# The opening of the first attention: the mask pattern made by TensorE instead of through DRAM, and a new order for mask copies, head moves, norms and loads

## The chip, the core and the metric

The kernel runs on one core of a Trainium2 chip. A core has a matrix engine (TensorE, PE in the profile; its weight loads are shown as PEld), three engines for elementwise work (VectorE or DVE, ScalarE or ACT, GpSimd or POOL) and SyncE (SP), which here only issues DMAs. Each engine runs its own queue in order; semaphores order the queues among each other. POOL issues DMAs too, in the same queue as its arithmetic. The metric is the device time of one execution in microseconds; before the change its median is 1165.69 us over three runs.

## The reference, cut to what matters

Two attention layers and two gated layers alternate, all with a residual around a layer norm without parameters. The change touches the first attention only.

```python
B, S, D = 1, 2048, 576;  H = 32;  Dh = 18;  W, dil = 8, 2
def attention(x, wqkv, wo):
    q, k, v = split_heads(layernorm(x) @ wqkv)
    idx  = pos[:, None] - arange(W)[None, :] * dil     # 8 keys per query, every second row back
    mask = idx >= 0
    logits = einsum('bhsd,bhswd->bhsw', q, k[idx]) * Dh**-0.5
    attn = softmax(where(mask, logits, -1e9))
    return (einsum('bhsw,bhswd->bhsd', attn, v[idx])) @ wo
def gated(x, w_in, w_sp, b_sp, w_out):                 # F = 4608
    z = gelu(layernorm(x) @ w_in);  z1, z2 = halves of z
    return (z1 * (w_sp @ layernorm(z2) + b_sp)) @ w_out
x = x + attention(x);  x = x + gated(x);  x = x + attention(x);  x = x + gated(x)
```

## The kernel before, in words

*Rows.* The even rows come first and the odd rows after them (`rows_of`), so a window of eight keys with dilation 2 is eight neighbouring rows. The 2048 rows are 16 row tiles of 128. For the attention they are cut anew into 17 query tiles: one of 128 and sixteen of 120, each with 8 rows of halo before it as keys.

*Projections.* `PG(d, qk, cc, ...)` computes 128 columns of q or k (column block d from 0 to 4; block 4 has q and k together) for 512 rows (row block cc from 0 to 3), five matmuls of 512 columns. The result is evicted into a stage buffer (`stg`, `lent`) that holds q and k of one column block for 1024 rows. When the stage is full, one DMA for each head moves its 18 rows to its place in `QK`, a tile in which four heads lie in the four groups of 32 partitions, eight such groups `g` one after another. These head moves go round the queues of POOL and SP, two to POOL for each on SP in the usual pattern `q2`. `VW(t, hh, ...)` computes half of the values of query tile t, five matmuls of 288 columns.

*Mask.* The 14 spare partitions behind the 18 of each head in `QK` carry a pattern (rows of codes and signs times a large number) for which the product of q and k is very negative outside the window. So one matmul gives masked logits. The pattern has a period of 128 rows, and a different start for the first 8. `build_window_rows` (L115) makes it: POOL fills a scratch tile `R` with constants, DVE computes the bits of the codes and writes them into `R`, three DMAs (`part1`, `part2`) store it to a small DRAM tensor `win_period`, and four DMAs (`load`, L184) read it back transposed into `win_pat`. `fill_window_rows` (L194) copies `win_pat` over one half of the rows of `QK` with four DVE copies of 4096 elements per partition, and two small ones for the start. The copies write all partitions, so a head's move must follow the copy of its place.

*The opening* (L597 to L727, with `li == 0`) is an order written out by hand, engine by engine as the calls stand in the code. `S_` takes the statistics of a row tile on DVE, `R_` the inverse root (an addition on DVE, a power on POOL), `A_` applies the norm on DVE into one of four buffers `ln_xn`. Tiles 0 to 3 are then transposed by TensorE (`T_pe`, L657) with an eviction on ACT, tiles 4 to 15 by a DMA transpose issued on SP (`ln_T`). 46 matmuls of the identity with itself keep TensorE at work until the first tile is there. Projections of row block 0 and of row block 1 follow, with the first values; ACT evicts them.

*The loop.* A step s is a half tile: eight groups of heads, half 0 with heads 0 to 15, half 1 with 16 to 31. `L_mm(s + 1)` computes 16 logits tiles, `EXP` exponentiates them on ACT, `PV(s)` multiplies by the values, and DVE divides by the sums into one of three buffers `o_t`, which a DMA transpose on SP turns (into `oT` or `o_slot`). A table says which projection, value, output product (`WO`), store, statistic and norm stands in which step. Projections of row blocks 2 and 3 that do not stand ahead of the loop (`pre`) are spread over its first steps, one in each; output products begin in step 13. There POOL takes over the norms of the 16 new row tiles (`LN_POW`, `LN_XN`), whose results the gated layer reads. `load_win2a` loads weights of the gated layer into space that was lent to two stages, and so waits for their moves.

## Time and profile before

| | |
|---|---|
| three runs | 1164.6, 1165.69, 1165.92 us; median 1165.69 |
| span of the profiled execution | 1170.2 us, 4.5 us above the median of the runs; its time outside the span is not shown |
| busy | PE 98%, PEld 52%, DVE 47%, ACT 29%, POOL 24% |
| opening | 0 to 44.8 us, when the first logits start |
| loop of the first attention | 50.75 (second half tile) to 126.4 us |
| first gated layer | from 126.4 us |
| DMA share of 16 engines | 0.92 until 12.65, 0.96 from 50.75 to 85.54, 1.07 from 85.54 to 126.4 |

How to read it: in a timeline each row has the start and the length in microseconds, the engine, the line of the kernel, what is written from what, how many instructions were merged, and in brackets the idle time of that engine just before and what ended it. Lines are those of the kernel before. A "q" behind an engine's name is its queue issuing a DMA. The time of a DMA from issue to landing is given for POOL's moves only.

### The profile page before, as it was taken

To read this page: it belongs to the slowest core of one execution; us is meant where nothing else is said; L and a number is where in the kernel's file an instruction comes from. 1 tells how busy PE (TensorE), PEld (TensorE's weight loads), DVE (VectorE), ACT (ScalarE), POOL (GpSimd) and SP (SyncE) were. 2 spreads that over 40 slices of the span, in tenths; PEclk is the share of its full clock that TensorE was granted. 3 is DMA by queue.
4 is the path that set the end of the run, shared out by engine and by line. 5 is a ranking of instruction groups with operands and counts; after the bars stand their busy time and mean duration, and the time that the engine had idled before them with its cause. 6 is when DMAs were issued, how large, how long until landed. Compare 5 with 4: busy or idle time off the path is not lost.

```text
span 1170.2 us, 19968 instructions
## 1 busy us (share of the span) xinstructions
PE 1150.5 (98%) x8163; PEld 612.5 (52%) x8258; DVE 550.0 (47%) x1167; ACT 338.8 (29%) x493; POOL 278.8 (24%) x389
## 2 busy tenths in 40 slices
PE   9999999999999999999999999999999999999998
PEld 5457544444444444457755774444444444444677
DVE  8668598322333332244555886963322223322321
ACT  5589455111100111101247884541011110111000
POOL 4659865000000000001153786640000000000000
PEclk9999999999999999999999999999999999999999
DMA  9599697000000000049646997930000000001332
GB/s 217 119 160 294 193 212 142 23 12 12 12 1 12 12 12 1 6 138 296 169 107 105 204 256 182 242 91 1 12 12 12 12 12 1 12 1 46 111 105 74
DMA packets 183240, 106.45 MB, mean 91 GB/s; under 512 B 135225, under 2 KB 164441, under 8 KB 183149
## 3 DMA queue, kind: packets, MB, share of 16 engines
q1 hardware_dynamic: 170285, 84.85, 31.6%
q0 software_dynamic: 6512, 14.57, 4.8%
q10 hardware_dynamic: 6352, 5.75, 1.6%
q8 instruction: 64, 1.05, 0.4%
q14 instruction: 27, 0.22, 0.1%
HBM read 42.40 MB, written 21.77 MB: 55 GB/s over the span
## 4 chain that ended last, share of the span: by engine, by line
PE 85%; POOL 7%; DMA 3%; DVE 2%; issue 2%; ACT 0%; SPq 0%; POOLq 0%; DVEq 0%; ACTq 0%
PE pg L1055 42%; PE po L1104 12%; PE pz L1031 6%; PE pz1s L1031 6%; PE pzs L907 5%; PE pp L436 4%; PE pz L907 4%; POOL ln_xn L259 4%; PE pv L410 2%; PE O_ps L496 1%; PE pw L557 1%; PE L_ps L473 1%; POOL ln_rstd L582 1%; DMA QK<-stg 1%; DMA o_slot<-o_t 1%
## 5 line engine op out<-in xcount | busy, mean ns | idle before, releaser
L1055 PE MATMUL pg<-Wq,Z 128*128 128x512 bf16 x2260 | 497.9, 379 | 2.5
L1055 PEld LDWEIGHTS <-Z 128*128 128x128 bf16 x2304 | 225.5, 98 | 271.8
L1059 DVE TENSOR_TENSOR g_tmp<-pg,ln_xn 128x512 f32<-128x512 f32 x144 | 99.6, 692 | 421.5 <-PE pg L1055 419.5
L1050 ACT ACTIVATE z1T<-pz 128x1024 bf16<-128x1024 f32 x36 | 34.9, 1021 | 500.8 <-PE pz L1031 500.8
L78 POOL DMA_DIRECT2D wout<-in_B_w_out_dram x4 | 4.3, 1070 | 598.8 <-PE pg L1055 598.8
L1104 PE MATMUL po<-wout,Z 128*128 128x288 bf16 x1152 | 141.4, 286 | 0.0
L482 ACT ACTIVATE P_sb<-L_ps 128x1440 bf16<-128x1440 f32 (+3 forms) x136 | 125.1, 972 | 21.1 <-PE L_ps L473 19.7
L1104 PEld LDWEIGHTS <-Z 128*128 128x128 bf16 x1152 | 112.7, 98 | 28.8
L907 PEld LDWEIGHTS <-xnT 128*128 128x128 bf16 (+1 forms) x800 | 68.7, 98 | 80.0 <-issue 15.5
L1060 DVE TENSOR_TENSOR Z<-g_tmp,z1T 128x512 bf16<-128x512 f32 x144 | 99.7, 692 | 12.2
L956 DVE BATCH_NORM_STATS2 z_st<-zp 128x6 f32<-128x512 bf16 (+1 forms) x160 | 91.0, 617 | 5.1 <-ACT zp L954 4.8
L1031 PEld LDWEIGHTS <-w 128*128 128x128 bf16 (+1 forms) x640 | 53.7, 97 | 74.0 <-issue 13.6
L436 PE MATMUL pp<-xnT,wqk_sb 128*128 128x512 bf16 x341 | 82.2, 382 | 2.5 <-DVE o_t L504 1.3
L259 POOL TENSOR_SCALAR ln_xn<-x_new,ln_mv,ln_rstd 128x576 bf16<-128x576 f32 x32 | 73.3, 2291 | 2.6
L1114 DVE TENSOR_TENSOR x_new<-po,xo 128x288 f32<-128x288 f32 (+1 forms) x64 | 28.8, 455 | 87.4 <-PE po L1104 83.9
L1031 PE MATMUL pz<-xnT,w 128*128 128x512 bf16 (+1 forms) x316 | 66.3, 380 | 0.2
L1031 PE MATMUL pz1s<-xnT,w 128*128 128x512 bf16 (+1 forms) x310 | 64.9, 379 | 0.9 <-issue 0.8
L78 POOL DMA_DIRECT2D QK<-stg x81 | 49.5, 614 | 46.0 <-DVE oT L524 14.8
L907 PE MATMUL pzs<-win2a,xnT 128*128 128x512 bf16 (+1 forms) x235 | 59.9, 364 | 0.4 <-issue 0.3
L907 PE MATMUL pz<-win2a,xnT 128*128 128x512 bf16 (+1 forms) x233 | 58.3, 357 | 0.6 <-issue 0.2
L980 POOL TENSOR_SCALAR Z<-zp,z_mv,z_rstd 128x256 bf16<-128x256 bf16 x32 | 55.7, 1740 | 3.4
L436 PEld LDWEIGHTS <-wqk_sb 128*128 128x128 bf16 x360 | 33.5, 98 | 38.3 <-DVE o_t L504 1.5
(113 smaller groups left out, 936.6 us busy)
## 6 DMA issues: line engine op xcount, KB each, us to landing
xres<-x_new SPq DMA_DIRECT2D x48, 288.0 KB
xo<-xres SPq DMA_DIRECT2D x32, 288.0 KB
wout<-in_B_w_out_dram POOLq DMA_DIRECT2D x4, 1296.0 KB, 8.2
xn_rows<-ln_xn SPq DMA_DIRECT2D x32, 160.0 KB
w<-in_B_w_in_dram SPq DMA_DIRECT2D x16, 256.0 KB
QK<-stg POOLq DMA_DIRECT2D x55, 72.0 KB, 5.2
xo<-xres SPq DMA_DIRECT2D x6, 576.0 KB
QK<-stg SPq DMA_DIRECT2D x39, 72.0 KB
```

What stands on the lines that cost most here:

```text
L78: return eng.dma_start(out=out, in_=in_)
L259: e.tensor_scalar(out=xn[:nrows, 0:D], in0=x_t[:nrows, :], scalar1=mv[:nrows, 0:1], scalar2=rstd[:nrows, 0:1], op0=ALU.subtract, op1=ALU.mult)
L436: nc.tensor.matmul(pp[:, :], lhsT=w, rhs=self.xnT[:, c, cc * 512:(cc + 1) * 512], start=(c == 0), stop=(c == 4))
L482: nc.scalar.activation(out=P_bufs[2 * jp + s % 2][:nk, :, :, 0:nq], in_=Lv[:nk, :, :, 0:nq], func=ACT.Exp, scale=scale)
L907: nc.tensor.matmul(out[:, o0:o0 + n], lhsT=self.xnT[r0:r1, c, r * P:(r + 1) * P], rhs=win2(c)[r0:r1, w0:w0 + n], start=start, stop=stop, t ...
L956: nc.vector.bn_stats(out=st[:, x // 512, :], in_=zp[:, x:x + min(512, w0 + n - x)])
L980: eng.tensor_scalar(out=Z[:, b0:b1, i, :], in0=zv[:, b0:b1, :], scalar1=mv[:, 0:1], scalar2=rstd[:, 0:1], op0=ALU.subtract, op1=ALU.mult)
L1031: nc.tensor.matmul(outs[a_], lhsT=w1[r0:r1, c, sub * P:(sub + 1) * P], rhs=self.xnT[r0:r1, c, q * 512:(q + 1) * 512], start=start, stop=st ...
L1055: nc.tensor.matmul(pg[:, :], lhsT=Z[:, jj, i, sub * P:(sub + 1) * P], rhs=Wq[q][:, i, :], start=(i == 0), stop=(i == NS - 1))
L1059: nc.vector.tensor_tensor(out=tmp[:], in0=pg[:, :], in1=bsp[:, qs], op=ALU.add)
L1060: nc.vector.tensor_tensor(out=uT(jj)[:, sub, qs], in0=tmp[:], in1=z1Ts[jj, sub][:, qs], op=ALU.mult)
L1104: nc.tensor.matmul(acc[hh], lhsT=u_rows(j, i), rhs=wouts[j // NJH][:, j % NJH, hh * 288:(hh + 1) * 288], start=(j == 0), stop=(j == NJ - 1))
```

## The change

What it does, part by part:

- The scratch `R` is laid out with 32 rows per head group, zeros included, and prepared on DVE and POOL (`base`). DVE still computes the bits; the codes are now written by POOL (`codes`, eight short operations), the signs are applied by ACT (`signs`).
- No DRAM tensor any more. `turn` (48 matmuls of up to 16 columns against the identity) transposes `R` into PSUM in the place of the first logits' tile, `turned` copies it out with ACT to 32 partitions (in a buffer that later holds probabilities), `spread_` repeats it over 128 partitions with two matmuls against a replicator matrix, and ACT copies it to `win_pat`. `turn` stands behind the transposes of tile 0, `spread_` behind the second projection group.
- The zeroing of weight rows goes from DVE to POOL. There are 44 warm-up matmuls instead of 46. Tile 1 is normalized by ACT instead of DVE; tile 3's transposes are evicted by DVE.
- The q and k weights and the rows 512 to 1023 are loaded in turn, k's weights first, and the first projections are those of k.
- The six copies of the first half of the mask stand between the norms and statistics of tiles 4 to 11, the four of the second half (which stood in `pre`) behind the statistics of tiles 14 and 15. The power of the root of tiles 10 and 11 now follows, on POOL, the head moves of column block 0, and that of tiles 12 to 15 follows those of block 1.
- The projections of row block 0 are done for k and q in turn as the weights come, those of block 1 after values 2 and 3. The first logits stand behind the values of tile 4 and ahead of those of tiles 5 to 8, which DVE evicts; three projection groups instead of six stand ahead of the loop, so the loop holds 15 instead of 12, two of them in step 0 and the last in step 13 instead of 11.

```diff
 def build_window_rows(self, c, R, rep, pat32):
-        one = self.dram.tile([2, MR, 2 * P + 8], bf16, name="win_period")
...
+        def codes():
+            e = nc.gpsimd
+            e.tensor_tensor(out=uu[:], in0=vf[:, 0:4, 0:2], in1=vf[:, 0:4, 1:3], op=ALU.add)
+            e.tensor_scalar(out=Rf[:, 0, 8:12, :], in0=vf[:, 0:4, 1:2].to_broadcast([P, 4, 16]), scalar1=half, ...)
...
+        def signs():
+            nc.scalar.activation(out=Rf[:, :, 0:8, :], in_=Rf[:, :, 0:8, :], func=ACT.Copy, scale=vf[:, 4, 1:2])
+        def turn(ps):
+            for a in range(2):
+                for b_ in range(2):
+                    for m in range(8):
+                        nc.tensor.matmul(ps[0:32, a, b_ * P + m:(b_ + 1) * P:8], lhsT=R[0:16, a, b_, m, :],
+                                         rhs=self.ident[0:16, 0:16], start=True, stop=True)
+                for m in range(8):
+                    nc.tensor.matmul(ps[0:32, 2, a * 8 + m:a * 8 + m + 1], lhsT=R[32:33, a, 0, m, :],
+                                     rhs=self.ident[32:33, 32:33], start=True, stop=True)
+        def turned(ps):
+            for a in range(2):
+                nc.scalar.copy(out=pat32[:, a, 0:2 * P], in_=ps[0:32, a, 0:2 * P])
+            nc.scalar.copy(out=pat32[:, :, 2 * P:], in_=ps[0:32, 2, 0:16].rearrange("p (a m) -> p a m", a=2))
+        def spread_(ps):
+            for a in range(2):
+                nc.tensor.matmul(ps[:, a, 0:2 * P + 8], lhsT=rep[0:32, :], rhs=pat32[:, a, :], start=True, stop=True)
+                nc.scalar.copy(out=pat[:, a, :], in_=ps[:, a, 0:2 * P + 8])
...
             self.load_wv(nc.sync, 2)
-            x_load(x1[:, 0:4, :], 4, 4, nc.sync)
-            self.load_wqk(nc.sync)
+            self.load_wqk(nc.sync, (0,))
+            x_load(x1[:, 0:2, :], 4, 2, nc.sync)
+            self.load_wqk(nc.sync, (1,))
+            x_load(x1[:, 2:4, :], 6, 2, nc.sync)
+            self.load_wqk(nc.sync, (2,))
             x_load(spare, 8, 4, nc.sync)
...
             S_(0)
             R_(0, 1)
-            S_(1)
-            R_(1, 1)
+            SB(1)
             A_(0)
             T_pe(0)
+            turn(X0)
...
+            PG(0, 1, 0, False)
+            PG(1, 1, 0, False)
+            spread_(X0)
+            F0[0]()
             A_(6, 7)
             T_(6, 7)
-            self.load_pat(nc.sync)
-            S_(9, 10, 11)
-            R_(8, 4)
+            setup_bufs(nc.gpsimd)
+            self.zero_right(nc.gpsimd, ("wo",))
             for f in self.load_win2a(nc.gpsimd)[4:6]:
                 f()
-            S_(12)
-            A_(8, 9, 10, 11)
-            T_(8, 9, 10, 11)
-            self.fill_window_rows(QK, 0)
-            S_(13, 14, 15)
-            order = [(d, 0) for d in range(4)] + [(d, 1) for d in range(4)] + [(4, 0), (4, 1)]
...
+            for d, qk in ((2, 1), (3, 1), (0, 0), (1, 0), (2, 0), (3, 0)):
+                PG(d, qk, 0, False)
+            S_(8, 9)
+            R_(8, 2)
+            F0[1]()
+            A_(8, 9)
+            T_(8, 9)
+            for f in F0[2:]:
+                f()
+            S_(10, 11)
+            RE(10, 2)
+            S_(12, 13)
+            for t in (2, 3):
+                for hh in range(2):
+                    VW(t, hh, False)
+            q2 = (nc.gpsimd, nc.sync, nc.gpsimd)
+            for d in range(4):
+                for qk in (1, 0):
+                    PG(d, qk, 1, False, q2)
+                if d == 0:
+                    RP(10, 2)
+                    A_(10, 11)
+                    S_(14, 15)
+                    RE(12, 4)
+                    for f in F1:
+                        f()
+                if d == 1:
+                    T_(10, 11)
+                    RP(12, 4)
+            PG(4, 0, 0, False, (nc.gpsimd, nc.sync))
+            PG(4, 0, 1, False, (nc.gpsimd, nc.sync))
+            A_(12, 13, 14, 15)
             T_(12, 13, 14, 15)
-            nvw0, nvw = 4, 9
+            VW(4, 0, False)
+            VW(4, 1, False)
+            self.ring = ["PT"]
+            L_mm(0)
+            EXP(0)
+            nvw0, nvw = 5, 9
...
-        pre, pgs = pgs[:6], pgs[6:]
+        npre = 3 if li == 0 else 6
+        pre, pgs = pgs[:npre], pgs[npre:]
         if li == 0:
-            pgs.insert(0, pgs.pop(-2))
+            pgs.insert(3, pgs.pop(-2))
         for k_, (d, qk, cc) in enumerate(pgs):
-            at(k_ if li == 0 else (k_ * PG_END) // len(pgs), PG, d, qk, cc, True, *((q2,) if li == 0 else ()))
+            at(max(0, k_ - 1) if li == 0 else (k_ * PG_END) // len(pgs), PG, d, qk, cc, True, *((q2,) if li == 0 else ()))
```

`RE` is the addition on DVE and `RP` the power on POOL that `R_` did together; `SB` and `SA` are the two parts of `S_`; `F0` and `F1` are lists of the copies that `fill_window_rows` made in one go, for the first and the second half of the rows.

222 lines of the change are left out of this document (113 added, 109 removed).

## The prediction

> **What bounds the kernel now.** I read the page's chain first, then the table of windows over the first attention layer, then the timelines of TensorE, DVE and POOL there.
>
> ```profile
> span 1170.2 us, 19968 instructions
> PE 85%; POOL 7%; DMA 3%; DVE 2%; issue 2%; ACT 0%; SPq 0%; POOLq 0%; DVEq 0%; ACTq 0%
> ```
>
> TensorE bounds the kernel; everything but TensorE on the chain is a place where it had nothing to do. The change touches the opening and the first attention, so I cut those into stages (columns: stretch in us, length, busy time and count of PE, PEld, DVE, ACT, POOL, granted clock, DMA share, GB/s):
>
> ```profile
> 36.50:39.00 2.50, 0.03 (x1) 0.00 (x0) 1.87 (x6) 0.00 (x0) 2.50 (x5) 1.00 0.69 170
> 39.00:44.80 5.80, 5.58 (x28) 2.94 (x32) 1.83 (x4) 0.80 (x2) 5.80 (x11) 0.71 0.74 168
> 50.75:85.54 34.79, 31.76 (x614) 18.84 (x620) 25.14 (x62) 30.11 (x34) 18.40 (x33) 1.00 0.96 137
> 149.00:153.00 4.00, 4.00 (x15) 1.55 (x15) 3.97 (x9) 2.31 (x4) 2.89 (x4) 0.57 0.59 123
> ```
>
> A TensorE that idled 2.5 us gets a granted clock of 0.71 for the next 5.8 us, which costs 0.29 x 5.8 = 1.7 us more; the loop of 34.79 us holds 3.03 us of idle. TensorE's timeline says where (start, length, last bracket the idle before it and what ended it):
>
> ```profile
> 6.43 0.45 PE L661 MATMUL pt<-ident,ln_xn 128*128 128x128 bf16 x5
> 7.70 0.45 PE L661 MATMUL pt<-ident,ln_xn 128*128 128x128 bf16 x5 [0.81 <-DVE ln_xn L654]
> 10.18 0.79 PE L661 MATMUL pt<-ident,ln_xn 128*128 128x128 bf16 x10 [0.19 <-DVE ln_xn L654]
> 12.65 8.80 PE L436 MATMUL pp<-xnT,wqk_sb 128*128 128x512 bf16 x39
> 21.29 1.39 PE L410 MATMUL pv<-wv_sb,xnT 128*128 128x288 bf16 x10
> 22.51 10.96 PE L436 MATMUL pp<-xnT,wqk_sb 128*128 128x512 bf16 x49
> 39.00 2.72 PE L410 MATMUL pv<-wv_sb,xnT 128*128 128x288 bf16 x15 [2.47 <-DVE v_ext L402]
> 51.08 0.56 PE L496 MATMUL O_ps<-v_ext,P_sb 128*128 128x19 bf16 x16
> 56.58 0.39 PE L473 MATMUL L_ps<-QK 32*128 32x120 bf16 x16
> 58.50 0.39 PE L473 MATMUL L_ps<-QK 32*128 32x120 bf16 x16
> 69.69 1.25 PE L436 MATMUL pp<-xnT,wqk_sb 128*128 128x512 bf16 x5 [0.74 <-DVE o_t L504]
> 74.28 1.25 PE L436 MATMUL pp<-xnT,wqk_sb 128*128 128x512 bf16 x5 [0.60 <-DVE o_t L504]
> 84.83 0.55 PE L473 MATMUL L_ps<-QK 32*128 32x120 bf16 x3 [0.43 <-DMA QK<-stg]
> 147.94 1.37 PE L907 MATMUL pzs<-win2b,xnT 64*128 64x512 bf16 x5 [0.97 <-ACT zp L954]
> ```
>
> Three places count: the 2.47 us before 39.00, the logits at 84.83 that wait for head moves of the second half of the rows, and 147.94, where the wait of 0.97 us is followed by the clock of 0.57. Behind the first stand DVE and POOL:
>
> ```profile
> 25.28 4.63 DVE L198 COPY QK<-win_pat 128x4096 bf16<-128x4096 bf16 x4 [2.05 <-DMA win_pat<-win_period]
> 30.04 0.81 DVE L641 BATCH_NORM_STATS2 ln_st<-x_in 128x6 f32<-128x288 bf16 x2
> 31.02 0.77 DVE L641 BATCH_NORM_STATS2 ln_st<-x_in 128x6 f32<-128x288 bf16 x2
> 37.13 1.45 DVE L654 TENSOR_SCALAR ln_xn<-x_in,lnx_mv,lnx_rstd 128x576 bf16<-128x576 bf16 x4 [3.92 <-POOL lnx_rstd L647]
> 15.46 0.72 POOL L647 TENSOR_TENSOR lnx_rstd<-lnx_rstd,neg_half 128x2 f32<-128x2 f32 x1 [0.58 <-DVE lnx_rstd L646]
> 30.85 5.20 POOL L78 DMA_DIRECT2D QK<-stg  x9 [7.84 <-DVE ln_st L641]
> 36.06 1.03 POOL L647 TENSOR_TENSOR lnx_rstd<-lnx_rstd,neg_half 128x4 f32<-128x4 f32 x1
> 37.06 3.60 POOL L78 DMA_DIRECT2D QK<-stg  x6
> ```
>
> The mask pattern reaches DVE at 25.28 after two trips through DRAM; the head moves may only follow the mask copies, so POOL's first starts at 30.85; the root of the last four tiles stands behind nine move issues on POOL, and DVE, which waits 3.92 us for it, evicts TensorE's value tiles late. Behind the other two places stands POOL again:
>
> ```profile
> 82.27 0.51 POOL L78 DMA_DIRECT2D QK<-win2a  x1 [2.63 <-DMA QK<-stg]
> 85.07 0.58 POOL L78 DMA_DIRECT2D win2a<-in_B_w_in_dram  x1 [0.68 <-DMA QK<-stg]
> 85.67 0.60 POOL L582 TENSOR_TENSOR ln_rstd<-ln_rstd,neg_half 128x1 f32<-128x1 f32 x1
> 145.71 1.76 POOL L980 TENSOR_SCALAR Z<-zp,z_mv,z_rstd 128x256 bf16<-128x256 bf16 x1
> ```
>
> From 85.67 to 147.47 POOL normalizes the sixteen tiles nearly without a pause, and its end releases ACT and TensorE at 147.94. POOL could not start earlier: its queue was stuck behind moves that waited for earlier ones to land. So what the change is worth at the layer's end is read from when POOL gets past those moves, not from TensorE's opening alone.
>
> **The change part by part.** Prices: eight projection groups take 21.29 - 12.65 = 8.64, so 1.08 each; two value halves 22.51 - 21.29 = 1.22, so 0.61 each; one tile's statistics 31.02 - 30.04 = 0.98; a norm 1.45 / 4 = 0.36; a POOL issue 5.20 / 9 = 0.58; a mask copy 4.63 / 4 = 1.16; a loop step with one group 58.50 - 56.58 = 1.92. The head moves' landings, first those issued from 30 to 46, then from 70 to 90:
>
> ```profile
> DMA to landing us min/median/max: 3.1/3.7/4.3
> ...
> DMA to landing us min/median/max: 5.4/7.9/8.5
> ```
>
> *Pattern turned.* 48 small matmuls come onto TensorE. The trace has none with 16 rows in and 16 columns out; the nearest row is the one at 51.08 (a weight load and 19 columns each): 0.56 / 16 = 35 ns, so 1.7 us. From above, 48 pairs at the warm-up's pitch would be 5.1 us:
>
> ```profile
> 1.36 4.93 PE L626 MATMUL warm<-ident 128*128 128x128 bf16 x46 [1.36 <-POOL ident L191]
> ```
>
> [...] Not below 48 x 24 ns = 1.2, the logits' 0.39 / 16 at 56.58, which run four abreast. I take 1.7, the row with the likest shape. The two spread matmuls of 264 columns cost half a 512-column matmul each, 0.2; two warm-ups fewer give 0.2 back. *Codes on POOL:* eight short operations now stand before the root of tile 0; at 0.2 us each (estimate: a third of the 0.60 that the root of one column takes at 85.67) they fill 1.6 us from the codes' arrival at about 4.0 and hold that root up by some 0.3, so the first transposes (6.43) slip by 0.3; at 0.6 each it would be 3 us, which I keep for the upper end. The turn lies in the idle of 0.81 before the second transposes, and the 0.19 before the third goes too. Sum of the opening: 1.7 + 0.2 - 0.2 + 0.3 - 1.0 = +1.0 us. ACT takes six small copies, the signs and one norm, some 3 us, beside evictions of 0.59 in each 1.08; the zeroing moves from DVE to POOL, which idled 2.11 before a root: both hide, and what they would cost uncovered is their own 3 and 1 us.
>
> ```profile
> 13.93 0.59 ACT L404 CAST stg<-pp 128x512 bf16<-128x512 f32 x1 [0.68 <-PE pp L436]
> 8.89 0.70 POOL L647 TENSOR_TENSOR lnx_rstd<-lnx_rstd,neg_half 128x2 f32<-128x2 f32 x1 [2.11 <-DVE win_vf L163]
> 13.88 6.71 SPq L266 DMA_TRANSPOSE xnT<-ln_xn  x4
> ```
>
> The loads are cut and reordered on SP with the same bytes; before, nothing waited for them at 12.65, so I cost them at nothing, between -0.2 and +0.5. Four loads and three stores of the pattern vanish from SP and POOL. The transposes of tiles 4 to 7 (6.71 on SP then) go out from about 16, so they are in by 23.
>
> *Mask copies and moves.* Two value halves move behind the first eight groups, so those start at 12.65 + 1.0 - 1.2 = 12.4 and, with the spread and four value halves (2.4), the second column block starts at 23.7. Its first two groups end at 25.9, are evicted by 26.6. DVE has by then, from 12.4, evicted a transposed tile (0.7, as ACT's 0.59 for 512 columns), done six statistics (5.9), six norms (2.2) and the mask copies (4.9): it ends at 26.1, so the copies no longer hold the moves. POOL then issues in order: five moves of block 0 (2.9), the root of tiles 10 and 11 (0.72), five of block 1 (2.9), the root of tiles 12 to 15 (1.03), then block 2. That last root also needs DVE: two norms 0.7, two statistics 1.95 after 30.2, so 33.0 against POOL's own 33.1: a tie. The second move of block 2 (head 15) starts at 26.6 + 2.9 + 0.7 + 2.9 + 1.0 + 0.6 = 34.7 and lands 3.7 later, 38.4.
>
> *New wait.* The first logits now stand ahead of eight value halves and three groups, and need heads 0 to 15 whole. TensorE is there at 25.9 + 8 x 1.08 + 1.22 = 35.8 and waits until 38.4: 2.6 us, in place of 2.47. Everything on TensorE is queued behind it. The same idle should bring the same clock loss, 1.7. DVE's four second-half copies (4.6) and last norms (1.4) end at 39.0, so its value evictions fit behind. The second logits come 0.3 + 8 x 0.61 + 3 x 1.08 + 1.7 = 10.1 later, at 48.5; before, they stood at 50.75 with three groups more done, so at 47.5 like for like: +1.0, the opening's sum; the removed stall is paid back by the new one.
>
> *Loop.* The three groups go into it: 31.76 + 3.24 = 35.0 us to the seventeenth half-tile, 83.5 if nothing waits. The output transposes now stand ahead of the moves on SP, so I let DVE's stalls (0.74, 0.60 and smaller) go. The moves of block 3, which that half-tile needs, follow step 12 instead of 10: 48.5 + 3.0 + 11 x 1.92 + 1.9 + 0.9 = 75.4, against 75.1 before. Their landing is then 7.9 and 8.5 as now, less perhaps 1 us because the output weights load before the queues fill. So the logits clear at about 84.7 (85.54 before), after a wait of 1.2, and POOL starts its sixteen tiles at about 84.9 instead of 85.67. TensorE has 0.97 in hand at the layer's end.
>
> **Sum:** 0.8 us less. On the profiled span 1170.2 that is 1169.4; the span lies 4.5 above the median of the runs, 1165.69, so 1164.9.
>
> **The rivals.** *Faster:* the first logits wait under a microsecond (moves landing at 3.1, POOL's chain 1 us shorter), and the clock stays. Then the loop starts at 48.5 - 1.6 - 1.7 = 45.2, block 3's moves 3.3 earlier, and POOL with them, of which I leave 0.6 to the full DMA queues: 0.8 + 3.3 - 0.6 = 3.5 less, 1162.2. For it: the loop's waits of 0.74 and 0.60 left its clock at 1.00. Against it: POOL's twelve issues in series. [...]
>
> *Slower, POOL shut out by the copies.* Four second-half copies of 1.16 now run on DVE exactly while POOL does the last root and block 2's issues. In the trace before POOL idles in both sets of copies, so no row shows them side by side; POOL's six issues beside DVE's norms took 3.60, 0.60 each, against 0.58. If POOL stood still in three of the four, head 15 would land 3.5 later, the second logits stand at 52.0, block 3's moves start at 78.9, and the end is 3.5 - 0.8 = 2.7 above before: 1168.4. It decides from 3.1 us of delay, where the end is 2.3 above. [...]
>
> *Slower, the turn is dear:* 48 at 107 ns are 3.4 more, so the end is 3.4 - 0.8 = 2.6 above before, 1168.3; if the narrow matmuls also let the clock fall, 1.7 more, 1170.0.
>
> *No effect:* the DMA queues (share 0.96 over the loop) hold 85.5 whatever precedes: 1165.7, inside my forecast.
>
> **Chances.** Forecast 0.40 (its own range 1163.4 to 1168.0), faster 0.30, shut out 0.18, dear turn 0.10, others 0.02. About 0.2% (2.3 us) is what a measurement of this kernel can tell from no change: faster by more 0.33, within 0.37, slower by more 0.30. The range reaches to both sides' cases: 1161.2 to 1169.5.
>
> **What will show it.** The turn's busy time on TensorE (1.7); the idle before the first logits and what ended it (2.6, a head move); clock below 1 in the 5 us behind; POOL's issues beside the second-half copies (0.58, or over 1 us if shut out); the wait of the seventeenth half-tile (1.2); POOL's first root of the loop (84.9); the wait at the layer's end. Wrong: if head 15 lands before TensorE gets there, or if POOL's loop start differs by over 2 us.

## The result, and the profile after

The changed kernel takes 1180.26 us (median of four runs, 1178.99 to 1182.6) against 1165.81 us for the kernel before beside it: a ratio of 1.0112, with a 95% interval from 1.0092 to 1.0132. That is 13.1 us (0.0112 x 1165.81) slower, where I had forecast 1164.9 and a range that ended at 1169.5.

The profiled execution of the changed kernel took 1178.99 us, its span 1177.2. The first lines of the page and the shares of the chain:

```profile
span 1177.2 us, 20161 instructions
PE 1160.6 (99%) x8306; PEld 614.8 (52%) x8306; DVE 555.4 (47%) x1174; ACT 338.9 (29%) x493; POOL 285.7 (24%) x390
...
PE 89%; POOL 6%; DVE 2%; DMA 1%; issue 1%; ACT 0%; SPq 0%; POOLq 0%; DVEq 0%; ACTq 0%
```

TensorE has more of the chain (89% against 85%), POOL a little less: the new time is spent where TensorE sets the pace, or where it works at a lower clock. The table over the stretches with a low clock, the first logits and the loop (columns as in the prediction):

```profile
9.80:13.20 3.40, 3.40 (x27) 2.49 (x22) 2.73 (x7) 2.07 (x4) 2.52 (x4) 0.50 1.12 306
40.58:45.54 4.96, 1.29 (x17) 0.55 (x17) 3.69 (x7) 1.52 (x2) 4.96 (x8) 0.84 0.77 137
43.94:50.76 6.82, 5.72 (x24) 3.50 (x25) 1.91 (x5) 1.94 (x2) 6.59 (x12) 0.50 0.85 159
56.66:91.13 34.47, 34.08 (x624) 19.58 (x617) 26.42 (x64) 29.71 (x33) 18.44 (x34) 1.00 0.76 123
730.00:733.40 3.40, 3.40 (x10) 1.28 (x9) 3.37 (x8) 1.78 (x3) 2.22 (x4) 0.50 0.69 158
```

There are three places at a granted clock of 0.50: one window of 3.4 us behind the opening's idle, two (6.82 us) at the first logits, and one at 730, in the layer behind the second attention, which the change doesn't touch. The loop is nearly free of idle (34.47 - 34.08 = 0.39 us). TensorE's timeline at the places of the prediction:

```profile
8.45 0.45 PE L704 MATMUL pt<-ident,ln_xn 128*128 128x128 bf16 x5 [2.02 <-DVE ln_xn L697]
8.83 0.48 PE L185 MATMUL L_ps<-ident,oT 16*32 16x16 bf16 x13
9.87 1.38 PE L426 MATMUL pv<-wv_sb,xnT 128*128 128x288 bf16 x5
15.01 2.32 PE L452 MATMUL pp<-xnT,wqk_sb 128*128 128x512 bf16 x10
18.28 0.27 PE L198 MATMUL L_ps<-P_sb,oT 32*128 32x264 bf16 x1 [0.74 <-ACT win_pat L199]
28.47 10.95 PE L452 MATMUL pp<-xnT,wqk_sb 128*128 128x512 bf16 x50 [0.89 <-DMA xnT<-ln_xn]
40.58 0.35 PE L489 MATMUL L_ps<-QK 32*128 32x128 bf16 x12
41.87 0.50 PE L489 MATMUL L_ps<-QK 32*128 32x128 bf16 x2 [0.94 <-DMA QK<-stg]
44.02 0.28 PE L489 MATMUL L_ps<-QK 32*128 32x128 bf16 x1 [1.65 <-DMA QK<-stg]
45.32 0.28 PE L489 MATMUL L_ps<-QK 32*128 32x128 bf16 x1 [1.02 <-DMA QK<-stg]
56.32 0.40 PE L489 MATMUL L_ps<-QK 32*128 32x128 bf16 x16
```

And DVE's and POOL's, first in the opening, then around the head moves:

```profile
7.96 0.43 DVE L697 TENSOR_SCALAR ln_xn<-x_in,lnx_mv,lnx_rstd 128x576 bf16<-128x576 bf16 x1 [1.47 <-POOL lnx_rstd L680]
5.09 0.63 POOL L162 TENSOR_SCALAR oT<-win_vf 128x64 bf16<-128x64 f32 x1
5.80 0.61 POOL L164 TENSOR_SCALAR oT<-win_uu 128x64 bf16<-128x64 f32 x1
7.35 0.58 POOL L680 TENSOR_TENSOR lnx_rstd<-lnx_rstd,neg_half 128x1 f32<-128x1 f32 x1
38.29 4.63 DVE L207 COPY QK<-win_pat 128x4096 bf16<-128x4096 bf16 x4
31.70 3.03 POOL L78 DMA_DIRECT2D QK<-stg  x5 [5.03 <-DVE ln_st L665]
38.49 2.20 POOL L680 TENSOR_TENSOR lnx_rstd<-lnx_rstd,neg_half 128x4 f32<-128x4 f32 x1
40.37 5.15 POOL L78 DMA_DIRECT2D QK<-stg  x6
45.52 5.01 POOL L78 DMA_DIRECT2D QK<-win2a  x9
91.13 0.60 POOL L598 TENSOR_TENSOR ln_rstd<-ln_rstd,neg_half 128x1 f32<-128x1 f32 x1
```

The codes hold the root of tile 0 until 7.35, DVE and TensorE wait for it, and the clock falls behind that wait. The moves start at 31.70, not at 26.6. Beside DVE's second-half copies (38.29 to 42.9) the root of four columns takes 2.20 us instead of 1.03 and a move's issue 5.15 / 6 = 0.86 instead of 0.58. POOL's moves end at 50.5 (45.52 + 5.01), and its first root of the loop is at 91.13, 5.5 us behind the 85.67 of before.

The spans of the two profiled executions differ by only 7.0 us, the runs by 13.1. So one question of the experiments was where the first layer's loss comes from, and another where the rest is.

### The profile page after: what moved, and what is told of

Same layout as the page of the kernel before. It is cut to its first block, busy times and chain, and to the rows that moved or that the text cites. A ratio compares the mean times of both kernels' runs of the same rounds, so it can differ in the third digit from the quotient of the medians.

```text
span 1177.2 us, 20161 instructions
## 1 busy us (share of the span) xinstructions
PE 1160.6 (99%) x8306; PEld 614.8 (52%) x8306; DVE 555.4 (47%) x1174; ACT 338.9 (29%) x493; POOL 285.7 (24%) x390
## 3 DMA queue, kind: packets, MB, share of 16 engines
q8 instruction: 65, 1.06, 0.4%
## 4 chain that ended last, share of the span: by engine, by line
PE 89%; POOL 6%; DVE 2%; DMA 1%; issue 1%; ACT 0%; SPq 0%; POOLq 0%; DVEq 0%; ACTq 0%
PE pg L1122 42%; PE po L1171 12%; PE pz L1098 6%; PE pz1s L1098 6%; PE pp L452 5%; PE pzs L974 5%; PE pz L974 4%; POOL ln_xn L275 3%; PE pv L426 3%; PE O_ps L512 2%; PE pw L573 2%; PE L_ps L489 1%; DMA QK<-stg 1%; POOL ln_rstd L598 1%; POOL QK L78 1%
## 5 line engine op out<-in xcount | busy, mean ns | idle before, releaser
L426 PE MATMUL pv<-wv_sb,xnT 128*128 128x288 bf16 x340 | 53.4, 300 | 0.0
```

What stands on the lines that cost most here:

```text
L426: nc.tensor.matmul(pv[:nk, 0:288], lhsT=self.xnT[:, c, k0_(t):k0_(t) + nk], rhs=wv_sb[:, c, hh * 288:(hh + 1) * 288], start=(c == 0), stop ...
```

## The experiments

Ratios are to runs of the kernel before on the same chip, with their 95% interval. "First root" is the start of POOL's first root in the first attention's loop, the number of the prediction that stands for the first layer.

**Three suspects in the changed kernel, one at a time.** My first theories were the codes on POOL (A), the second-half copies beside POOL (B) and the lack of cover behind the first logits (C).

```diff
         def codes():
-            e = nc.gpsimd
+            e = nc.vector
...
-            codes()
             signs()
...
             A_(0)
+            codes()
             T_pe(0)
             turn(X0)
```

> The eight code operations go from POOL, ahead of tile 0's root, to DVE, behind tile 0's norm. Theory A (these operations, 0.2 to 0.6 us each on POOL, hold the root of tile 0 up and so cause the idle of 2.02 us and the half clock behind it): the root starts near 5.0 instead of 7.35, the first transposes at 6.4 to 6.7 instead of 8.45, no granted clock of one half near 9.8, the first projection at 11.5 to 12.6 instead of 15.01, and the run is 2 to 4 us shorter than the changed kernel. Rival (DVE is the late one there: eight operations more on it hold the statistics up, and the turn waits for them): first transposes at 6.5, but idle of 1 us or more before the turn and behind it, first projection not before 13.5, end 0 to 1.5 us shorter.

Measured: ratio 1.0071 [1.0047, 1.0095]; first transposes at 6.95, but first projection only at 14.51, and first root at 90.14. TensorE's timeline in this kernel: the idle before the transposes fell from 2.02 to 0.53 us.

```profile
6.95 0.45 PE L703 MATMUL pt<-ident,ln_xn 128*128 128x128 bf16 x5 [0.53 <-DVE ln_xn L696]
...
10.23 0.71 PE L703 MATMUL pt<-ident,ln_xn 128*128 128x128 bf16 x5 [0.82 <-ACT ln_xn L693]
```

And yet the clock behind it, in the table over 9.70 to 13.00:

```profile
9.70:13.00 3.30, 2.77 (x18) 2.15 (x19) 2.40 (x6) 2.14 (x5) 2.50 (x5) 0.50 1.12 300
```

It was halved all the same. A holds for the root and misses the projection, which the rival has. At the first logits TensorE, 0.6 us earlier, waits 4.0 us instead of 3.6, and the second logits stand at 56.11 instead of 56.32: what the opening gave was lost there. The runs are 4.1 us shorter by their medians (1176.2 against 1180.26) and the first root only 1.0; the two intervals overlap, and where the rest would come from is not shown.

```diff
                     RE(12, 4)
-                    for f in F1:
-                        f()
...
             A_(12, 13, 14, 15)
             T_(12, 13, 14, 15)
+            for f in F1:
+                f()
```

> The four mask copies of the second half go on DVE from ahead of the last four norms to behind them. Theory B (a copy on DVE shuts POOL out): the root of tiles 12 to 15 takes 1.0 to 1.1 us instead of 2.20, the first issues of block 2 take 0.58 each instead of 1.1 to 1.5, head 15's move starts near 40.3 and lands near 43.4 instead of 45.3; first logits whole 1.8 to 2.2 us earlier; the end 1.8 to 4 us shorter (the larger value if one window of half clock goes with it). Rival (the landing is set by the DMA queues, which are fed from two issuers): issues shorten, but head 15 lands at 45 all the same, end within 0.7 us of the changed kernel.

Measured: ratio 1.0088 [1.0043, 1.0133], first root 90.75. POOL's timeline:

```profile
39.40 1.03 POOL L680 TENSOR_TENSOR lnx_rstd<-lnx_rstd,neg_half 128x4 f32<-128x4 f32 x1
40.40 3.52 POOL L78 DMA_DIRECT2D QK<-stg  x6
43.91 7.63 POOL L78 DMA_DIRECT2D QK<-win2a  x9
```

The root is back at 1.03 and the six issues at 0.59 each; the nine behind them, which now run beside the copies, take 0.85 each instead of 0.56. So B's effect is shown, but it only moved along the queue. In this execution the opening was 1.1 us later (clock low from 8.32 to 15.15), and the last of the first logits, at 46.32 instead of 45.32, gained nothing. The same root took 2.20 us beside the copies and 1.03 away from them, longer by about one copy (4.63 / 4 = 1.16).

```diff
-            self.ring = ["PT"]
-            L_mm(0)
-            EXP(0)
             nvw0, nvw = 5, 9
...
-                VW(t, hh, li == 0)
+                VW(t, hh, False)
...
-            if k_ == 0 and li > 0:
+            if k_ == 0:
```

> The first logits go back behind the eight value halves of tiles 5 to 8 (which ACT evicts now, since DVE is still busy with copies). Theory C (the wait for head 15 is a matter of cover: 4.9 us of value work lie right behind it): no wait of over 0.5 us at the first logits, no half clock from 44 to 51, second logits at 49 to 50 instead of 56.32, POOL's first root of the loop 5 to 7 us before 91.13, end 5 to 7.5 us shorter than the changed kernel. Rival (POOL's sixteen normalizations are held by the DMA queues in the loop, not by TensorE's progress): second logits early, but waits for moves appear in the loop, and POOL's first root comes no more than 2 us earlier.

Measured: ratio 1.0108 [1.0077, 1.0139], first root 89.42. The first logits ran without a wait, at 45.27, and the second ones took their place. Two of their five waits on TensorE's timeline:

```profile
52.43 0.31 PE L489 MATMUL L_ps<-QK 32*128 32x128 bf16 x2 [0.76 <-DMA QK<-win2a]
53.41 0.42 PE L489 MATMUL L_ps<-QK 32*128 32x128 bf16 x2 [0.68 <-DMA QK<-win2a]
```

And the table over the stretch behind them:

```profile
54.56:57.97 3.41, 3.41 (x9) 1.06 (x7) 1.21 (x3) 1.05 (x2) 0.00 (x0) 0.50 0.37 125
```

With a granted clock of 0.50 there, C is right for the one place, and worth 1.7 us at the first root, not 5 to 7 (the runs show no gain clear of their intervals): the whole stream of moves is late, and here the next logits waited for it.

The three edits together, that is the three diffs above:

> The three edits together (codes on DVE behind tile 0's norm, second-half mask copies behind the last norms, first logits behind the value halves). If A, B and C hold and add up to where other work binds: first projection near 12, second logits at 45 to 46.5, POOL's first root of the loop at 80 to 83, end 9 to 12 us below the changed kernel, that is 3 us above to 3 us below the kernel before, since before it stood like for like at 47.5. Rival (the loop's DMA queues bind): second logits at 45 to 47, but POOL's first root at 85 to 86, as in the kernel before, end within 1 us of before.

Measured: ratio 1.0086 [1.0066, 1.0107], first root 89.01 instead of 80 to 83. All three theories together explain 2.1 of the 5.5 us. They had to be replaced.

**The narrow turn and the clock.** In the kernel with the codes on DVE, the body of the turn:

```diff
-                        nc.tensor.matmul(ps[0:32, a, b_ * P + m:(b_ + 1) * P:8], lhsT=R[0:16, a, b_, m, :],
-                                         rhs=self.ident[0:16, 0:16], start=True, stop=True)
...
+            for k_ in range(12):
+                nc.tensor.matmul(ps[:, a, j * P:(j + 1) * P], lhsT=self.ident[:], rhs=self.ident[:], start=True, stop=True)
```

> The kernel with the codes on DVE, in which twelve matmuls of 128x128 stand in the place of the turn's 48 narrow ones; the mask pattern isn't computed, so the mask rows are wrong. With the codes on DVE the idle before the first projection had shrunk to 0.53 and 0.82 us, and the half clock from 9.68 to 13.09 stayed. Theory A2 (the narrow matmuls of the turn, 16 rows by 16 columns, count as idle for the clock): no granted clock of one half before 15 us, first projection at 12.6 to 13.3 instead of 14.51. Rival (the idle of 0.5 and 0.8 us does it): half clock at the same place, first projection at 14 or later. For the end both theories say little, since the moves behind it are late for another reason: 0 to 2 us below the kernel with the codes on DVE.

Measured: ratio 1.0064 [1.0048, 1.0080], first projection 13.77, first root 90.09. No half clock in the opening, although TensorE idled longer than with the narrow turn. Its timeline:

```profile
6.95 0.45 PE L698 MATMUL pt<-ident,ln_xn 128*128 128x128 bf16 x5 [0.81 <-DVE ln_xn L691]
7.24 0.83 PE L184 MATMUL L_ps<-ident 128*128 128x128 bf16 x12
...
10.21 0.45 PE L698 MATMUL pt<-ident,ln_xn 128*128 128x128 bf16 x5 [1.24 <-ACT ln_xn L688]
```

And the same stretch of the table, with the clock at 1.00:

```profile
9.70:13.00 3.30, 2.38 (x26) 1.81 (x27) 2.38 (x6) 3.04 (x8) 2.50 (x5) 1.00 1.12 309
```

All four runs have a mean clock of 0.997, against 0.994 to 0.996 with the narrow turn. With the narrow turn, TensorE was busy for 2.60 of the 3.41 us ahead of the half clock:

```profile
6.26:9.67 3.41, 2.60 (x60) 1.84 (x58) 3.23 (x17) 1.15 (x3) 1.13 (x4) 1.00 1.01 300
```

That is more than the 2.38 of 3.30 us at which the wide turn kept its clock. So in this pair the half clock goes with the turn's narrow matmuls, on top of short waits, and not with TensorE's busy time. The projection was 0.5 us later than expected, for the longer waits. Again the opening's gain doesn't reach the loop.

**The order and the turn, each alone.** Theory D: the order cuts the stream of head moves. First the changed opening with the order of before from tile 8 on (the loop's own lines are those of before too):

```diff
             T_(6, 7)
+            spread_(X0)
+            S_(9, 10, 11)
+            R_(8, 4)
...
+            A_(8, 9, 10, 11)
+            T_(8, 9, 10, 11)
+            for f in F0:
+                f()
+            S_(13, 14, 15)
+            order = [(d, 0) for d in range(4)] + [(d, 1) for d in range(4)] + [(4, 0), (4, 1)]
```

> The changed kernel's opening with the turned pattern, but from tile 8's statistics on the order of the kernel before (norms of tiles 8 to 11 ahead of the first mask copies, second-half copies and the last value halves behind the fourth group of block 2, six groups ahead of the loop). Theory D (the late end comes from the order: roots on POOL, transposes on SP and the second-half copies cut the stream of head moves, which runs from 31.4 to 50.5 instead of from 30.2 to 45.7): the moves issue without a pause but for one root, from 30 to 46; POOL's first root of the loop at 86 to 87.5 instead of 91.13; end 3 to 5 us below the changed kernel. Rival (the loss is made in the opening, where TensorE's second column block starts at 28.5 instead of 22.5, and stays): POOL's first root at 90 or later, end within 1.5 us of the changed kernel.

Measured: ratio 1.0078 [1.0060, 1.0097]; the first root at 86.53, as D has it; POOL's moves start at 32.96, later than expected, with one root between them, and end at 49.96, hardly before the 50.53 of the changed kernel. The first logits ran at 45.26 without a wait, the second ones waited 0.97 us. The runs gained 4.0 us on the changed kernel (0.0034 x 1166), within D's 3 to 5, but are still 9.1 us (0.0078 x 1166.6) slower than the kernel before.

Then the opening of before with the changed order:

```diff
+            for d, qk in ((0, 1), (1, 1), (2, 1), (3, 1), (0, 0), (1, 0), (2, 0), (3, 0)):
+                PG(d, qk, 0, False)
+            S_(9)
+            R_(8, 2)
+            A_(8, 9)
+            T_(8, 9)
+            for f in F0:
+                f()
+            S_(10, 11)
...
```

From there to the end of the loop it is as the changed kernel.

> The opening of the kernel before (pattern through DRAM, its loads), with the changed kernel's order from tile 8's norms on: copies and moves ahead of the norms of tiles 10 to 15, second-half copies beside the moves, first logits ahead of the value halves, three groups ahead of the loop. Theory D: the stream of moves starts near 30.5 and ends near 49.5, and POOL's first root of the loop comes at 89 to 91 instead of 85.67, the end 3 to 5 us above the kernel before. Rival (the opening is the cause): POOL's first root at 87 or earlier, end at most 1.5 us above the kernel before.

Measured: ratio 1.0063 [1.0046, 1.0080], 7.3 us slower than the kernel before; first root 92.18, later than in the changed kernel. Its TensorE is at the first logits 3.5 us earlier than in the changed kernel and is through with them 1.3 us later. From its timeline:

```profile
37.10 0.63 PE L481 MATMUL L_ps<-QK 32*128 32x128 bf16 x7
39.23 0.46 PE L481 MATMUL L_ps<-QK 32*128 32x128 bf16 x3 [1.50 <-DMA QK<-stg]
...
46.59 0.28 PE L481 MATMUL L_ps<-QK 32*128 32x128 bf16 x1 [2.32 <-DMA QK<-stg]
```

The table over 40.41 to 50.65:

```profile
40.41:50.65 10.24, 5.19 (x23) 2.92 (x24) 4.67 (x10) 2.05 (x2) 9.98 (x16) 0.50 0.78 143
```

And POOL's timeline:

```profile
38.36 2.18 POOL L657 TENSOR_TENSOR lnx_rstd<-lnx_rstd,neg_half 128x4 f32<-128x4 f32 x1
40.23 5.15 POOL L78 DMA_DIRECT2D QK<-stg  x6
```

POOL has the same root at 38.4 and the same issues as in the changed kernel, whose TensorE came from a quite different opening: the stream of moves sets the end of these logits, and TensorE only waits more or less for it. The clock is at one half for 10.24 us, but TensorE was busy for only 5.19 of them, so that costs 2.6 at most; the rest is waiting. D stands as far as the whole order goes: alone it makes a first-layer loss as large as the changed kernel's. Which part of the order costs how much, these runs don't separate.

Then the turn with the order of before throughout, placed where it was meant to hide (the codes are on DVE; against the kernel before, cut):

```diff
             S_(3)
             R_(2, 2)
+            codes()
+            signs()
             A_(2, 3)
             T_pe(2)
             T_pe(3)
             VW(1, 1, False)
+            turn(X0)
+            turned(X0)
...
                 PG(d, 1, 0, False)
+                if d in (1, 2):
+                    spread_(X0, (d - 1,))
                 PG(d, 0, 0, False)
```

> Order of the kernel before throughout, with the pattern turned by TensorE: codes on DVE where they stood before, the turn behind tile 1's last value half, the two spread matmuls a group apart so that no copy of ACT is waited for. Theory D with A2: TensorE's second column block starts at 24 to 25 (22.5 before plus the turn's 1.0 and the spread's 0.5; 1.7 more if the turn costs the clock), the mask copies start at 23.5 instead of 25.3 and the moves at 28.5 to 29, the wait of 2.47 us before the values is under 0.7, the clock stays; the first step of the loop at 48.5 to 50 instead of 51.08; end 0 to 2.5 us below the kernel before. Rival (the head moves of block 3 and the full DMA queues hold the loop's middle whatever precedes): loop starts as early, but POOL's first root at 85 to 86 as before, end within 0.5 us of before; or, if the narrow turn halves the clock and the wait stays, 1 to 3 us above before.

Measured: ratio 1.0053 [1.0034, 1.0072], 6.2 us slower, although its first layer was better than that of the kernel before: no wait before the values, first root at 83.71. In its trace it is 3.6 us ahead of the profile before at 600, and level with it at 760. What it had won was lost from 690 on: 1.9 us by the last roots of the second attention, and 1.7 in a window of half clock from 722.84. In the opening the clock was at one half from 9.45 to 12.87, ahead of the turn, which starts at 13.94. The 3.41 us ahead of that window:

```profile
6.04:9.45 3.41, 1.58 (x19) 1.14 (x18) 3.27 (x12) 1.06 (x2) 1.06 (x2) 1.00 0.97 295
```

There is no narrow matmul in them, only waits of 1.01 and 0.82 us; so here the half clock came without narrow matmuls. The variant with less work ahead of tile 0 lost as much:

```diff
-            bits_()
...
             S_(0)
...
             A_(1)
+            bits_()
             T_pe(1)
...
+            for _ in range(12):
+                nc.tensor.matmul(warm[:, 0:P], lhsT=self.ident[:], rhs=self.ident[:], start=True, stop=True)
```

> The kernel with the turn hidden, with DVE's bit operations moved from ahead of tile 0's statistics to behind tile 1's norm, and twelve idle matmuls where TensorE waits for tiles 2 and 3. In the kernel with the turn hidden the first transposes stood at 7.32 behind idle of 1.01, the clock was half from 9.45 to 12.87 and the projections began at 16.22. Theory: first transposes at 6.3 to 6.6, no half clock before 20, projections from 14.0 to 14.8, POOL's first root of the loop at 82 to 83.3 instead of 83.71 (85.67 before), end 1.5 to 3.5 us below the kernel with the turn hidden, that is within 1.5 us of the kernel before or below it. Rival (DVE's chain of statistics and norms sets the mask copies and with them the moves, whatever TensorE does): projections earlier, but copies at 24.5 and moves at 29.5 as now, POOL's first root at 83.5 or later, end within 1 us of the kernel with the turn hidden.

Measured: ratio 1.0053 [1.0035, 1.0071], first root 83.37. No half clock in the opening, the first transposes at 6.43, but tiles 2 and 3 later, projections at 15.70: the rival has the copies and the end.

**The same two kernels again.** Both unchanged, for a second profile:

> The kernel before, unchanged, for a second profile. Its first profile has a span of 1170.2, while most of its runs take 1164.4 to 1167.2 at a mean clock of 1.0. Theory E (whether a wait of 0.8 to 2.5 us halves the clock for 3.4 us is chance, and so is the wait at the end of the second attention): this profile has no half clock at 40 or at 149, the second logits come 1.7 us earlier, the span is 1163 to 1167. Rival (the wait of 2.47 us always halves the clock): half clock from 40 on again, second logits at 50.7 again, and the difference of the runs lies elsewhere.

> The changed kernel, unchanged, for a second profile. Theory E for it: the idle of 2.02 us before the narrow turn and the 3.6 us at the first logits are long enough to halve the clock every time: half clock again near 9.8 and for two windows near 44, POOL's first root of the loop within 0.5 us of 91.13; only the third place, 730, may be gone. Rival (all is chance): one or more of the first two places without half clock, POOL's first root 1.5 us or more earlier.

Measured: the kernel before took 1169.27 us, with the half clock from 40.46 to 43.87 again behind a wait of 2.56 us, none at 149, and its first root at 84.65. The changed kernel took 1179.47, with two windows of half clock at the first logits again and its first root at 91.92. In the opening its transposes ran at half pace again, but this time from the first ones on (0.71 us for five at 8.45, where the first profile has 0.45), so ahead of the turn; the granted clock of this profile reads 1.00 from 8 to 15 all the same. Both places of the changed kernel come back in TensorE's pace, and in the kernel before the clock at 40 came back too; 149 and 730 did not. For 40 to 44 Theory E stays open: both profiles have the window, but of 29 runs of the kernel before beside the last kernels 15 have a mean clock of 1.0, which leaves none that the clock's record shows. The padded kernel below, nearly the same code, waited only 1.06 us there, kept its clock, and had its first root at 80.26.

The second profiles also divide the loss. Their spans differ by 10.2 us: 7.3 stand at the first root, 8.1 at the first root of the second attention's loop, 10.0 at its last.

**Where the other half is.** At the end of the second attention POOL waits for the last rows, whose stores go through DRAM. All profiles up to here with the turn in them, but that with the late copies, waited longer there. One thing of the change does reach so far: the turn adds 48 pairs of matmul and weight load to TensorE's code, with the spread and two warm-ups fewer some 100 instructions. The page counts a queue of kind "instruction" with 64 packets of 16 KB in the kernel before (1.05 MB) and 65 in the changed one; over the 8163 + 8258 matmuls and weight loads that the profile before counts that is one for 257 of them. Theory F: this queue brings TensorE's code, and 100 instructions more move every later fetch, and one of them into that wait. The test adds such instructions to the kernel before and does nothing else:

```diff
-            for _ in range(46):
+            for _ in range(61):
+                nc.tensor.matmul(warm[0:16, 0:16], lhsT=self.ident[0:16, 0:16], rhs=self.ident[0:16, 0:16], start=True, stop=True)
+            for _ in range(35):
                 nc.tensor.matmul(warm[:, 0:P], lhsT=self.ident[:], rhs=self.ident[:], start=True, stop=True)
```

> The kernel before with 100 TensorE instructions more and no other change: of its 46 warm-ups 35 stay, and 61 narrow ones of 16 rows and 16 columns, of about the same length together, stand ahead of them. Theory F (TensorE's code comes in 16 KB fetches, one for some 250 instructions of matmul and weight load; the turn's 100 instructions shift all later fetches, and at the end of the second attention one lands where stores of the last rows have to get through): the first layer as in the kernel before, but the code fetch at the end of the second attention moves into the wait behind the last rows (51 to 53 us after the first root of that loop instead of 47.7 and 60.7), the last two pairs of roots come 1 to 2 us later (57.3 to 58.5 instead of 56.5), the runs 2 to 5 us above the kernel before. Rival (chance): roots at 56.5, runs within 1 us of the kernel before.

Measured: ratio 1.0035 [1.0016, 1.0053]: 4.1 us slower (1.9 to 6.2), with the same work. The edit is not quite code alone: behind the narrow warm-ups the first five transposes took 0.74 us instead of 0.45. The profiled execution is one of the fastest of its twelve (1167.76 of 1167.49 to 1176.89), with its first root 4.4 us ahead of the second profile of the kernel before and its end only 1.5 us ahead. POOL's timeline at the last roots of that loop, with the wait before them:

```profile
703.48 1.08 POOL L582 TENSOR_TENSOR ln_rstd<-ln_rstd,neg_half 128x1 f32<-128x1 f32 x2 [7.38 <-DVE ln_rstd L581]
```

The queues that were busy in that wait (packets, MB, share of 16 engines):

```profile
q1 hardware_dynamic: 2532, 1.31, 65.4%
q8 instruction: 1, 0.02, 0.8%
```

The same two views of the kernel before, where no fetch falls into the wait:

```profile
707.77 1.08 POOL L582 TENSOR_TENSOR ln_rstd<-ln_rstd,neg_half 128x1 f32<-128x1 f32 x2 [5.04 <-DVE ln_rstd L581]
```

```profile
q1 hardware_dynamic: 1976, 0.87, 64.7%
```

And of the changed kernel, with a fetch in it:

```profile
712.84 1.08 POOL L598 TENSOR_TENSOR ln_rstd<-ln_rstd,neg_half 128x1 f32<-128x1 f32 x2 [6.77 <-DVE ln_rstd L597]
```

```profile
q1 hardware_dynamic: 1975, 1.34, 76.5%
q8 instruction: 1, 0.02, 1.6%
```

The counter-test takes 66 instructions out of the changed kernel, with the same warm-up work:

```diff
-            for _ in range(44):
-                nc.tensor.matmul(warm[:, 0:P], lhsT=self.ident[:], rhs=self.ident[:], start=True, stop=True)
+            for _ in range(11):
+                nc.tensor.matmul(warm[:].rearrange("p (r x) -> p r x", x=P), lhsT=self.ident[:],
+                                 rhs=self.ident[:, None, :].to_broadcast([P, 4, P]), start=True, stop=True)
```

> The changed kernel with 11 warm-ups of 512 columns in place of 44 of 128, the same work in 66 TensorE instructions less. Theory F: the first layer as in the changed kernel (POOL's first root of the loop at 91 to 92), but code fetches at the second attention's end back near 47 and 58 to 60, the roots there at 56 to 56.6 instead of 57.7 and 58.5, the runs 2 to 4 us below the changed kernel's 1179 to 1182. Rival (chance): the runs as the changed kernel's.

Measured: ratio 1.0075 [1.0056, 1.0093] instead of 1.0112: 4.3 us of the loss are gone, with the first layer no better (first root 92.95). The wait before the last roots, and the queues in it:

```profile
712.12 1.07 POOL L598 TENSOR_TENSOR ln_rstd<-ln_rstd,neg_half 128x1 f32<-128x1 f32 x2 [4.29 <-DVE ln_rstd L597]
```

```profile
q1 hardware_dynamic: 1534, 0.71, 59.5%
```

Over the 17 profiles of this study, that wait was 4.29 to 5.07 us in the seven without a fetch of this queue in it, and 6.41 to 7.77 us in nine of the ten with one (4.50 in the tenth, the kernel with the copies late). And a second loss follows: in six of the nine profiles with the longer wait a window of half clock begins between 706 and 731, worth 1.7 us (half of its 3.4), and in none of the eight others. F holds, as far as the shift of the code goes: three kernels moved by 4.1, 4.3 and 5.8 us (the third below) the way that it says, each with an uncertainty of 2 to 3 us. The padded kernel's trace itself shows 2.3 of its 4.1 us, in the wait; it has no such window. How the fetch lengthens the wait is not shown; what the profiles show is that the wait of another engine, with such a fetch in it, was 1.3 to 3.5 us longer in nine of ten.

The same trim, by the same lines, in the kernel with the turn hidden, and then with POOL's two selects on the pattern cut out of `base()` as a function of their own:

```diff
             R_(1, 1)
+            self.win_select()
             A_(0)
```

> The kernel with the turn hidden, its warm-ups trimmed in the same way. Theory F with D: first layer as that kernel's (POOL's first root of the loop near 83.7, 1 to 2 us ahead of the kernel before), no loss at the second attention's end, so the runs 0 to 3 us below the kernel before, where they were 6 above. Rival (chance there, or the profile of the first layer isn't typical): runs 3 us or more above the kernel before.

> The kernel with the turn hidden and the warm-ups trimmed, in which POOL's two selects on the pattern go behind the root of tile 1, so that DVE's bit operations aren't slowed beside them (one took 1.06 us instead of 0.28). Theory: tile 0's statistics start at 3.6 instead of 4.53, the first transposes at 6.4 instead of 7.32, no half clock before 15, projections from 14.0 to 14.6 instead of 16.22; POOL's first root of the loop at 82 to 83.3; runs 1 to 4 us below the kernel before. Rival (the mask copies and moves don't follow, as when the bit operations alone were moved): first root at 83.4 or later, runs within 1 us of the trimmed kernel.

Measured: ratios 1.0003 [0.9991, 1.0014] and 1.0001 [0.9989, 1.0014]; first roots at 85.12 and 81.94. The trim took away 5.8 us (1.0053 to 1.0003), and with it all that was left of the loss. But neither is faster than the kernel before. The first of them missed its first root of 83.7; its first transposes ran at half pace (0.71 us). The second has its first transposes at 6.68 and its projections only at 15.37. Its first root is 2.7 us ahead of the nearer profile of the kernel before, but both of those executions were slower than that kernel's median, so this is no gain in the runs. DVE's chain of statistics and norms has its mask copies start at 24.9 in the last of them, hardly before the 25.28 at which they could start with the pattern through DRAM, so there was little for the turn to win, and what I expected of the earlier selects (1 to 4 us below) did not come.

## Why the prediction was wrong

By its own sign the prediction failed in the first layer: POOL's first root of the loop stood at 91.13 instead of 84.9, 6.2 us off where it allowed 2. Most of the rest of the loss lies at the end of the second attention and just behind it, where it had no term at all.

The sum of the loss: the order alone is 7.3 us (5.4 to 9.3), the code shift alone 4.1 (1.9 to 6.2), and of the 13.1 measured (10.7 to 15.4) 1.7 would remain for the turn's opening. That is less than these intervals, and the parts don't simply add: the turn with the order of before is 9.1 us slower, 5.0 more than the code shift. The wait for the moves hides much of the opening's delay: with the order alone TensorE came to the first logits 3.5 us earlier and left them 1.3 us later.

*Pattern turned, as a price:* too dear in time, too cheap in effect. 48 matmuls took 9.87 - 8.83 = 1.04 us instead of 1.7, but the clock fell behind them. With the codes on DVE it fell behind the narrow matmuls (0.50) and not behind twelve wide ones in their place (1.00); in the changed kernel a wait of 2.02 us stands in front of them too, and the share of each is not shown. The rival of the dear turn (107 ns each, the warm-ups' 4.93 / 46, during which the granted clock reads 1.00) named that and gave it 1.7 us, which is what a window of 3.4 us at one half costs; I gave it one chance in ten.

*Codes on POOL:* 0.61 and 0.63 us for the two wide ones instead of 0.2, so the root came 2.4 us later, not 0.3. My upper end (0.6 each) held it. Eight operations of one engine don't have one price; I took that of a single column for 64. The first projection stood at 15.01 instead of 12.4.

*The second column block at 23.7:* it started at 28.47. The 2.6 us of the opening, 0.74 for ACT's copy between the two spread matmuls, which work on one PSUM tile, and 0.89 for the last transposes of these rows (SP issues them until 24.7) are 4.2 of these 4.8. I had costed the spread as matmuls only, and the transposes as in by 23.

*Copies no longer hold the moves, POOL in series:* this is the step that failed most. The rival "shut out" was right in its effect (a root of 2.20 us beside the copies instead of 1.03, the first three issues 1.1 to 1.5), and it came out on top of a stream that began 5 us later than I had it. What I had not seen is that the last move that the next logits need decides, not the first. The first logits need heads 0 to 15, whose moves come out of `stg`. In the kernel before, POOL had issued these by 40.66, with one root among them; in the changed kernel by 45.52, with two roots and the copies among them, while SP did the transposes of tiles 10 and 11 between its own. And the values and groups that covered this wait before now stand behind it: with the turn and the order of before the whole stream ended as late (49.96), but the first root came 4.6 us earlier. Later copies only slowed POOL's later moves (0.85 us an issue instead of 0.56), and the logits behind the values left the wait to the next logits.

*New wait of 2.6 us with the same clock loss of 1.7:* it was 0.94 + 1.65 + 1.02 = 3.6 us, and two windows with 5.72 us of work in them, so up to 2.9. "The removed stall is paid back by the new one" was the wrong sentence: the old one stands in front of work that the moves don't need and costs one window; the new one grows when TensorE gets there earlier (7.3 us of waiting with the order alone).

*Loop of 35.0 us without stalls:* nearly right. From the second logits at 56.32 to the seventeenth half-tile at 90.16 it is 33.8, and POOL's start follows that half-tile as I had it (after a wait of 0.73 instead of 1.2). But it began 7.8 us later than 48.5.

*The sum against the profiled execution:* I carried its 4.5 us over the median along as if it were in both. Part of it is clock: of 29 runs of the kernel before beside the last kernels, 15 have a mean clock of 1.0, which leaves no recorded window of 3.4 us at one half, while the four runs of the changed kernel show 0.994 to 0.996 (a window of 3.4 us at one half takes 1.7 / 1167 = 0.0015 off the mean). What I booked as the same 1.7 in both is there in every run of the changed kernel, and in the kernel before in some.

*What was not in it at all:* the code. I costed the turn's instructions on TensorE at their own time, beside what they delay there, and not as 100 instructions that stand in front of 16,000 others. The runs give it 4.1 us. No rival held that, and the range couldn't.

## What to carry to other kernels

A transfer stream that feeds the next stage is costed by the last transfer that this stage needs: list every instruction that its issuing queues do before that one, ask what waits for it rather than for the first, and which work stands ahead of that wait to cover it. The kernel before with 100 TensorE instructions more was 0.35% slower (4.1 us, 1.9 to 6.2) for the same work, and what its trace shows of it is a wait behind stores through DRAM, 7.38 us with a fetch of the "instruction" queue in it instead of 5.04 without one in the kernel before; so for a small loss far behind a change the places of these fetches are compared first. And a profile is one execution: before a stall's clock loss is booked on both sides, look whether the runs' mean clock says that it is there.

## What the runs showed of the hardware

- Narrow matmuls and the clock: with 48 matmuls of 16 x 16 or 1 x 1 among waits of 0.53 and 0.82 us the clock went to one half for 3.4 us; with twelve of 128 x 128 in their place among waits of 0.81 and 1.24 us it stayed at 1.00. In the last kernel the same narrow matmuls, 0.94 us of waiting and 1.3 us of wide ones behind the values, ran at 1.00 (the mean clock of that execution). The stretches at one half lasted 3.4 us (9.80 to 13.20 in the changed kernel, 40.46 to 43.87 in the second profile of the kernel before, 54.56 to 57.97 with the logits behind the values) or longer (6.82 us at the changed kernel's first logits, 10.24 with the order alone).
- Waits and the clock: at the same place of the kernel before, waits of 2.47 and 2.56 us cost a window, and one of 1.06 us in the padded kernel didn't. The length alone doesn't decide: in the two profiles of the changed kernel, TensorE waited 1.33 and 1.34 us at the same place near 730, and a window followed in the first only.
- DVE's mask copies and POOL: in the changed kernel a root of two columns took 1.55 us beside a copy (0.72 away from it), one of four 2.20 (1.03 with the copies late), a move's issue 0.86 on average (0.58 in the kernel before). The other way round, a small integer operation of DVE took 1.06 us beside POOL's selects (the kernel with the turn hidden) and 0.17 away from them (the last kernel).
- 100 TensorE instructions more, for the same work, cost 4.1 us of 1167 (1.9 to 6.2). What the traces show of it is some 700 us later: a wait of 4.3 to 5.1 us without a code fetch in it, 6.4 to 7.8 with one in nine of ten profiles.
